# Batch 1's query path in a fused attention and feed-forward kernel: casts moved, columns as 64 by 64 tiles, batch 2's queries cast by GpSimd and turned at another place

## The chip, the cores and the metric

The kernel runs on one core of one Trainium2 chip. The metric is the time of one execution on the device in microseconds (us). Engines: PE is TensorE's matmul, PEld its weight load, DVE is VectorE, ACT is ScalarE, POOL is GpSimd, SPq is the queue from which transfers are issued.

## The reference

Per batch (8 batches, 8 heads, 576 rows, 64 columns a head): linear attention, a norm of each head's row, then a gated feed-forward with a norm ahead.

```python
kv  = einsum('bhsd,bhse->bhde', k, v)              # a 64x64 state per head
out = einsum('bhsd,bhde->bhse', q, kv)
out = out / sqrt(mean(out*out, -1) + 1e-6) * g_norm
x   = out.transpose(0, 2, 1, 3).reshape(4608, 512)
xn  = x / sqrt(mean(x*x, -1) + 1e-6) * rms_g
y   = (silu(xn @ w_gate) * (xn @ w_val)) @ w_out   # 512 -> 1536 -> 512
```

## The kernel before

The feed-forward of batch n and the attention of batch n+1 are interleaved on TensorE. The "up parts" are the products with w_gate and w_val, the "down parts" those with w_out. Between the up parts of batch 0 and those of batch 1, the rows of batch 1 have to be made: states from k and v, queries cast to bf16 and turned (by TensorE against an identity), columns (state times queries) for the sums of squares, row products, the norm, the row scalings, and a turn of the scaled rows. The down parts of batch 0 are placed between these steps to fill TensorE. The order, with cuts marked:

```python
for c in range(4):
    down_part(c, 0, 2)
att1.kv_products()                                   # states, diagonal 64x64 tiles
for i, engine in enumerate((DVE, SC)):
    cast_q(1, slice(2 * i, 2 * i + 2), engine)       # heads 0..3
att1.kv_copy()                                       # waits for the states
clear_tail_rows(1, DVE)
for i, engine in enumerate((DVE, SC)):
    cast_q(1, slice(2 * i + 4, 2 * i + 6), engine)   # heads 4..7
for c in range(4):
    down_part(c, 2, 4)
turns.q_turn(0, SC); turns.q_turn(1, DVE)            # 8 turns each, then a copy
# ... GpSimd casts of w_out
for c in range(2):
    down_part(c, 4, 6)
for j in range(NS):
    f_cols(j)             # one 128x128 matmul of 512 columns, then a square (ScalarE, j == 1 VectorE)
for c in range(2, 4):
    down_part(c, 4, 6)
F.alloc_sums(); F.sums(); f_o(0); F.head(); F.root() # sums, row products, Newton steps on VectorE
# ... down parts 6 to 8 with f_o(1..3) between
down_part(0, 8, 12)
xs = [F.scale(c, F.outa[c]) for c in range(4)]       # VectorE, both inputs in SBUF
ffn.down_out(0)
down_part(1, 8, 12)
f_x(0, xs[0], SC); f_x(1, xs[1], SC)                 # turns of the scaled rows
ffn.down_out(1)
alloc_q(2); cast_q(2, slice(0, 4), SC)               # batch 2's queries
down_part(2, 8, 12)
f_x(2, xs[2], DVE); f_x(3, xs[3], DVE)
down_part(3, 8, 12)
ffn.down_out(2); ffn.down_out(3)                     # the second one issues two stores
cast_q(2, slice(4, 8), DVE)
# ...
for c in range(T):
    atts[2].q_rows(c)                                # transposing transfers, in the queue after the stores
```

Of the kernel before, what the change touches and what calls it, by code (L numbers as in the profile page):

```python
# [10 lines left out]
FP32 = mybir.dt.float32  # L11
# [4 lines left out]
OP = mybir.AluOpType  # L16
ACT = mybir.ActivationFunctionType
# [3 lines left out]
def kernel(  # L21
# [14 lines left out]
    B, H, S, D = q.shape  # L36
    d_model = H * D
# [4 lines left out]
    T = 4  # L42
    MAIN = 128 * T
    TAIL = S - MAIN
    NS = d_model // 128
# [7 lines left out]
    def pool(name, bufs, **kw):  # L53
        return ctx.enter_context(tc.tile_pool(name=name, bufs=bufs, **kw))
# [13 lines left out]
    osb_pool = pool("osb", 2)  # L68

    PS = bass.MemoryType.PSUM  # L70
    gps_pool = pool("gps", 2, space=PS)
    vps_pool = pool("vps", 2, space=PS)
    ops_pool = pool("ops", 2, space=PS)
    att_pool = pool("att", 2, space=PS)
# [3 lines left out]
    PE, DVE, SC, GP = nc.tensor, nc.vector, nc.scalar, nc.gpsimd  # L78

    identity = consts.tile([128, 128], BF16, name="identity")  # L80
# [3 lines left out]
    gsq = consts.tile([128, 1], BF16, name="gsq")  # L84
    rowscale = consts.tile([128, NS], FP32, name="rowscale")
    sel = consts.tile([128, 2, 2], BF16, name="sel")
# [3 lines left out]
    kv_all = consts.tile([128, B, NS, 128], BF16, name="kv_all")  # L90
# [13 lines left out]
    def cast(engine, dst, src):  # L104
        if engine is SC:
            engine.copy(out=dst, in_=src)  # L106
        else:
            engine.tensor_copy(out=dst, in_=src)  # L108
# [35 lines left out]
    def cast_kv(b, name, i, engine):  # L144

        if b < EARLY:
            cast(engine, pairs_buf(b, name)[:, i].rearrange("p c d -> p (c d)"), pairs_raw(b, name)[:, i, :])
        elif i < NS:
            hs = slice(2 * i, 2 * i + 2)
            src = raws[b, name][:, 0 : MAIN * T].rearrange("p (h t d) -> p t h d", h=H, t=T)  # L150
            cast(engine, bufs[b][name][:, 0:T, hs, :], src[:, :, hs, :])
        else:
            src = raws[b, name][0:TAIL, MAIN * T :].rearrange("r (h d) -> r h d", h=H)
            cast(engine, bufs[b][name][0:TAIL, T], src)
# [10 lines left out]
    def alloc_q(b):  # L165
        bufs[b]["q"] = qb_pool.tile([128, T, H, D], BF16, name="qb")

    def cast_q(b, hs, engine):
        src = raws[b, "q"].rearrange("p (h t d) -> p t h d", h=H, t=T)[:, :, hs, :]
        cast(engine, bufs[b]["q"][:, :, hs, :], src)  # L170
# [48 lines left out]
    def round_wo(blk, i, n, engine):  # L219
        c = 4 * blk + i  # L220
        cast(engine, wo_sb[:, c : c + n, :], w_st["o", blk][:, i : i + n, :])
# [61 lines left out]
    def clear_tail_rows(i, engine):  # L283

        for t in (kbs[i], vbs[i]):
            engine.memset(t[TAIL:128, T], 0.0)
# [10 lines left out]
    class Att:  # L297
# [77 lines left out]
        def sums(self, c):  # L375
            if c == 0:
                self.ssq = stat_pool.tile([128, T, 2, H], FP32, name="ssq")
            sq = self.sq[c // 2][:, c % 2]
            DVE.tensor_tensor(out=sq[:, 1], in0=sq[:, 0], in1=gsq8, op=OP.mult)  # L379
            DVE.reduce_sum(out=self.ssq[:, c], in_=sq, axis=AX.X)  # L380
# [30 lines left out]
    class Cols:  # L411
# [11 lines left out]
                ps, lhsT=kv_all[:, self.n, j, :], rhs=self.qt[:, j, self.lo : self.hi], start=True, stop=True  # L423
            )

        def square(self, j, ps):
            SC.activation(out=self.sq[:, j, :], in_=ps, func=ACT.Square)

        def alloc_sums(self):
            self.bank = att_pool.tile([128, 512], FP32, name="att_ps")  # L430
            self.st = self.bank[:, 0 : self.nc * 2 * H].rearrange("p (c i h) -> p c i h", c=self.nc, i=2)

        def sums(self):
            for c in range(self.nc):
                PE.matmul(self.st[:, c, 0, :], lhsT=ones, rhs=epsrow, start=(c == 0), stop=False, skip_group_check=True)
            for j in range(NS):
                for c in range(self.nc):
                    PE.matmul(
                        self.st[:, c, :, 2 * j : 2 * j + 2], lhsT=self.sq[:, j, 128 * c : 128 * c + 128], rhs=sel,
                        start=False, stop=(j == NS - 1 and c == self.nc - 1), skip_group_check=True,  # L440
                    )

# [160 lines left out]
    for j in (0, 1):  # L603
# [5 lines left out]
        out=gam[NS : NS + 1, :].rearrange("o (i d) -> o i d", i=2),  # L609
        in_=g_norm.rearrange("(o d) -> o d", o=1).unsqueeze(1).to_broadcast([1, 2, D]),  # L610
# [83 lines left out]
    def rows_banks():  # L694
        return [ops_pool.tile([128, MAIN], FP32, name="o_ps") for _ in range(2)]
# [12 lines left out]
    for j in (0, 1):  # L708
# [24 lines left out]
    squares(A, 0, banksA[0])  # L733
    columns(A, 2, banksA[1])
    square(A, 2, banksA[1])
    kv3 = state0(3, 1)
    DVE.scalar_tensor_tensor(
        out=gsq, in0=gcol, scalar=1.0 / d_model, in1=gcol, op0=OP.mult, op1=OP.mult
# [5 lines left out]
    warm(A.bank, 1)  # L744
    columns(A, 3, banksA[1])
    square(A, 3, banksA[1])
    warm(A.bank, 1)
    A.sums()
# [64 lines left out]
    def broadcast_gsq():  # L813
        ps = att_pool.tile([128, 512], FP32, name="att_ps")
        PE.matmul(
            ps[:, 0:D], lhsT=gsq[0:D, :].to_broadcast([D, 128]), rhs=identity[0:D, 0:D], start=True, stop=True
        )
        DVE.tensor_copy(out=gsq8, in_=ps[:, 0:D].unsqueeze(1).to_broadcast([128, H, D]))

# [7 lines left out]
    for i in range(2):  # L827
        banks = [b.rearrange("p (u t) -> p u t", u=2) for b in rows_banks()] if i == 0 else None
        ffn.gate_pair(i, 256, ffn.up_pair(i, 256, banks=banks))
    broadcast_gsq()  # L830
    for s in range(2):
        round_w(3, "g", s, SC)
# [23 lines left out]
    turns = Turns(1)  # L856
# [22 lines left out]
        round_wo(0, i, 1, GP)  # L879
    alloc_xnt(1)  # L880

    def f_cols(j):
        p, nm = ((att_pool, "att_ps"), (att_pool, "att_ps"), (gps_pool, "g_ps"), (vps_pool, "v_ps"))[j]
        ps = p.tile([128, MAIN], FP32, name=nm)
        F.turned(j, ps)
        if j == 1:
            copy = osb_pool.tile([128, 2, d_model], FP32, name="o_sb")[:, 0, :]
            DVE.tensor_copy(out=copy, in_=ps)
            DVE.tensor_tensor(out=F.sq[:, j, :], in0=copy, in1=ps, op=OP.mult)
        else:  # L890
            SC.activation(out=F.sq[:, j, :], in_=ps, func=ACT.Square)

    def f_o(c):
        F.o(c, att_pool.tile([128, H, D], FP32, name="att_ps"), SC)

    def f_x(c, x, engine):
        bank = att_pool.tile([128, NS, 128], BF16, name="att_ps")
        to_rows(x, 1, c, bank, engine)

    pools = ("ops", "ops", "g", "v")  # L900

    def down_part(c, lo, hi):
        ffn.down_products(c, lo, hi, pools[c])
# [5 lines left out]
    for c in range(4):  # L909
        down_part(c, 0, 2)  # L910
    att1.kv_products()
    for i, engine in enumerate((DVE, SC)):
        cast_q(1, slice(2 * i, 2 * i + 2), engine)
    att1.kv_copy()
    clear_tail_rows(1, DVE)
    for i, engine in enumerate((DVE, SC)):
        cast_q(1, slice(2 * i + 4, 2 * i + 6), engine)
    for c in range(4):
        down_part(c, 2, 4)
    turns.q_turn(0, SC)  # L920
    turns.q_turn(1, DVE)
    for blk in (1, 2):
        for i in range(4):
            round_wo(blk, i, 1, GP)
    F = Cols(1, 0, 512, turns.qt, sqt_pool.tile([128, NS, MAIN], BF16, name="sqt"), "F")
    for c in range(2):
        down_part(c, 4, 6)
    for j in range(NS):
        f_cols(j)
    for c in range(2, 4):  # L930
        down_part(c, 4, 6)
    F.alloc_sums()
    F.sums()
    f_o(0)
    F.head()
    F.root()
# [11 lines left out]
    f_x(0, xs[0], SC)  # L948
    f_x(1, xs[1], SC)
    ffn.down_out(1)  # L950
    alloc_q(2)
    cast_q(2, slice(0, 4), SC)
    down_part(2, 8, 12)
    f_x(2, xs[2], DVE)
    f_x(3, xs[3], DVE)
    down_part(3, 8, 12)
    ffn.down_out(2)
    ffn.down_out(3)
    cast_q(2, slice(4, 8), DVE)



# [18 lines left out]

    cast_kv(2, "k", 0, DVE)
    cast_kv(2, "k", 1, DVE)
    atts = {b: Att(b) for b in range(2, B + 1)}
    for c in range(T):
        atts[2].q_rows(c)

    for n in range(1, B + 1):
        ffn = Ffn(n)
        steps = {u: [] for u in range(NF + T)}  # L990
# [9 lines left out]
        if n < B:  # L1000
# [5 lines left out]
            for i in range(2):  # L1006
                u = kv0 + 1 + 2 * i
# [9 lines left out]
        b = n + 2  # L1017
# [53 lines left out]
```

## Time and profile before

| | before |
|---|---|
| median, first three runs | 321.22 us (321.01 to 322.49) |
| span of the profiled run | 319.0 us |
| TensorE busy | 308.9 us, 97% of the span |
| TensorE in the chain that ended last | 87% |
| GpSimd busy | 22.8 us, 7% |

TensorE is busy nearly everywhere, so the busy shares show no place to gain. The way to read such a profile is to lay the starts of successive matmul groups side by side and to look for the places where one group starts later than the groups before it explain.

### The profile page before, as it was taken

What the parts mean: (1) busy time and instruction counts of PE and PEld (TensorE: products, weight loads), DVE (VectorE), ACT (ScalarE), POOL (GpSimd) and SP (SyncE); (2) the same over time, 40 slices, a digit from 0 to 9 for tenths busy, and PEclk for the clock granted to TensorE, in tenths of its full rate; (3) what the DMA queues carried; (4) which work ended last, traced back from release to release, by engine and by line L of the source; (5) the groups of instructions that cost most, each with busy time, mean ns of one, the idle gap of its engine ahead of it and who ended that gap; (6) DMA issues with size and microseconds to landing.
All of it is one profiled execution on the core that took longest, in us unless ns stands there. A gap on an engine that the chain in (4) does not pass through costs nothing.

```text
span 319.0 us, 5591 instructions
## 1 busy us (share of the span) xinstructions
PE 308.9 (97%) x2138; PEld 151.3 (47%) x2175; DVE 181.4 (57%) x372; ACT 176.6 (55%) x313; POOL 22.8 (7%) x48
## 2 busy tenths in 40 slices
PE   7899999999999999999999999999999999999995
PEld 3585456444454444444444444444444444444443
DVE  4685757669438922893279417951796079604310
ACT  3677457475667466837683767366744374233321
POOL 1274341300000000000000000000000000000000
PEclk9999999999999999999999999999999999999999
DMA  7999999888389757924792499946002600230014
GB/s 267 361 386 386 376 373 302 197 249 207 66 161 303 167 136 191 313 56 111 191 320 71 79 185 222 322 86 197 2 0 57 183 27 1 56 144 0 0 35 99
DMA packets 72903, 54.90 MB, mean 172 GB/s; under 512 B 42280, under 2 KB 64044, under 8 KB 72876
## 3 DMA queue, kind: packets, MB, share of 16 engines
q1 hardware_dynamic: 72496, 53.88, 60.4%
q10 hardware_dynamic: 380, 0.66, 0.6%
q8 instruction: 17, 0.28, 0.4%
q14 instruction: 10, 0.08, 0.1%
HBM read 37.75 MB, written 9.44 MB: 148 GB/s over the span
## 4 chain that ended last, share of the span: by engine, by line
PE 87%; DMA 6%; SPq 2%; issue 1%; DVE 1%; another core or an unknown queue 1%; ACT 1%; POOL 1%
PE v_ps L493 27%; PE g_ps L493 27%; PE o_ps L535 26%; DMA st<-in_moe_w_val_dram 3%; DMA st<-in_q_dram 2%; PE att_ps L278 1%; SPq L319 1%; DMA qt<-qb 1%; PE v_ps L535 1%; PE g_ps L535 1%; DMA out_dram<-o_sb 1%; POOL wv_sb L207 1%; PE o_ps L510 1%; PE att_ps L357 1%
## 5 line engine op out<-in xcount | busy, mean ns | idle before, releaser
L499 DVE TENSOR_TENSOR h_sb<-silu,v_ps 128x512 bf16<-128x512 bf16 x104 | 71.2, 684 | 98.7 <-ACT silu L498 66.7
L493 PE MATMUL v_ps<-xnt,wv_sb 128*128 128x512 bf16 x409 | 106.1, 379 | 0.6
L493 PE MATMUL g_ps<-xnt,wg_sb 128*128 128x512 bf16 x398 | 104.6, 379 | 0.8 <-ACT wg_sb L205 0.2
L498 ACT ACTIVATE silu<-g_ps 128x512 bf16<-128x512 f32 x104 | 62.1, 597 | 72.7 <-PE g_ps L493 57.7
L535 PE MATMUL o_ps<-wo_sb,h_sb 128*128 128x512 bf16 x386 | 86.9, 379 | 0.5
L493 PEld LDWEIGHTS <-wv_sb 128*128 128x128 bf16 x416 | 40.7, 98 | 49.1
L535 PEld LDWEIGHTS <-h_sb 128*128 128x128 bf16 x420 | 40.7, 98 | 47.8
L493 PEld LDWEIGHTS <-wg_sb 128*128 128x128 bf16 x416 | 39.6, 98 | 46.4
L106 ACT COPY o_sb<-o_ps 128x512 f32<-128x512 f32 (+1 forms) x34 | 19.7, 579 | 38.1 <-PE o_ps L535 35.3
L106 ACT CAST vb<-st 128x512 bf16<-128x512 f32 (+2 forms) x30 | 17.2, 628 | 3.3 <-DMA st<-in_v_dram 3.3
L397 DVE TENSOR_TENSOR xna<-outa,s1y 128x512 bf16<-128x512 bf16 x28 | 17.9, 685 | 0.0
L380 DVE TENSOR_REDUCE ssq<-sqt 128x16 f32<-128x1024 bf16 x14 | 17.1, 1220 | 0.5
L380 DVE TENSOR_REDUCE ssq<-sq 128x16 f32<-128x1024 bf16 x14 | 17.1, 1220 | 0.5
L106 ACT CAST qb<-st 128x1024 bf16<-128x1024 f32 (+1 forms) x17 | 15.4, 943 | 1.1 <-DMA st<-in_q_dram 1.1
L106 ACT CAST kb<-st 128x512 bf16<-128x512 f32 (+1 forms) x25 | 14.0, 619 | 0.0
L366 ACT ACTIVATE sq<-att_ps 128x512 bf16<-128x512 f32 x14 | 7.6, 594 | 4.3 <-PE att_ps L357 3.6
L379 DVE TENSOR_TENSOR sq<-sq,gsq 128x512 bf16<-128x512 bf16 x14 | 5.9, 422 | 4.9 <-ACT sq L366 4.9
L635 PE MATMUL att_ps<-kv_all 128*128 128x512 bf16 (+1 forms) x21 | 7.2, 467 | 1.2 <-DVE sel L624 1.2
L108 POOL CAST wo_sb<-st 128x512 bf16<-128x512 f32 x12 | 7.1, 620 | 7.9 <-DMA st<-in_moe_w_out_dram 7.9
L366 ACT ACTIVATE sqt<-o_ps 128x512 bf16<-128x512 f32 x14 | 7.6, 598 | 0.0
L371 ACT CAST outa<-att_ps 128x512 bf16<-128x512 f32 x14 | 7.5, 593 | 0.0
L371 ACT CAST outa<-o_ps 128x512 bf16<-128x512 f32 x14 | 7.5, 593 | 0.0
(145 smaller groups left out, 181.7 us busy)
## 6 DMA issues: line engine op xcount, KB each, us to landing
out_dram<-o_sb SPq DMA_DIRECT2D x14, 512.0 KB, 2.9
st<-in_q_dram SPq DMA_DIRECT2D x6, 1024.0 KB, 7.0
st<-in_k_dram SPq DMA_DIRECT2D x6, 1024.0 KB, 10.3
st<-in_v_dram SPq DMA_DIRECT2D x6, 1024.0 KB, 11.9
st<-in_moe_w_out_dram SPq DMA_DIRECT2D x6, 512.0 KB, 11.0
st<-in_moe_w_gate_dram SPq DMA_DIRECT2D x4, 512.0 KB, 9.6
st<-in_moe_w_val_dram SPq DMA_DIRECT2D x4, 512.0 KB, 8.8
st<-in_k_dram SPq DMA_DIRECT2D x4, 288.0 KB, 4.3
```

Of the source, the lines that this page charges most:

```text
L106: engine.copy(out=dst, in_=src)
L108: engine.tensor_copy(out=dst, in_=src)
L366: SC.activation(out=self.sq[i][:, :, 0, g:H:2, :], in_=self.banks[i][g], func=ACT.Square)
L371: SC.copy(out=rows[:, :, g:H:2, :], in_=self.banks[i][g])
L379: DVE.tensor_tensor(out=sq[:, 1], in0=sq[:, 0], in1=gsq8, op=OP.mult)
L380: DVE.reduce_sum(out=self.ssq[:, c], in_=sq, axis=AX.X)
L397: DVE.tensor_tensor(out=self.xna[c], in0=self.outa[c], in1=self.alpha[:, c, :].to_broadcast([128, H, D]), op=OP.mult)
L493: PE.matmul(ps, lhsT=wt[:, s, j * 128 : (j + 1) * 128], rhs=x[:, s, :], start=(s == 0), stop=(s == NS - 1),)
L498: SC.activation(out=silu, in_=g_ps, func=ACT.Silu)
L499: DVE.tensor_tensor(out=self.h[:, j, :], in0=silu, in1=v_ps, op=OP.mult)
L535: PE.matmul(self.o_ps[c], lhsT=self.h[:, j, c * 128 : (c + 1) * 128], rhs=wo_sb[:, j, :], start=(j == 0), stop=(j == NF - 1),)
L635: PE.matmul(ps[:, 0:w], lhsT=warm_sb[:, 0:128], rhs=warm_sb[:, 0:w], start=True, stop=True, skip_group_check=True)
```

## The change

It is meant to take out the small waits of TensorE around batch 1's rows: queries are cast before the state copies; the two query turns are put between down parts; the columns are made of 64 by 64 tiles, four of which are meant to run at once; batch 2's queries are cast by GpSimd, and their turning transfers go ahead of the last two stores. Cut to its core:

```diff
+        def turned_tiles(self, i, banks):
+            for u in range(2):
+                out = slice(u * D, u * D + D)
+                for g in range(2):
+                    rows = slice(g * D, g * D + D)
+                    PE.matmul(banks[g][out], lhsT=kv_all[rows, self.n, 2 * i + u, rows],
+                              rhs=self.qt[rows, 2 * i + u, :], start=True, stop=True)
 ...
-    for i, engine in enumerate((DVE, SC)):
+    for i, engine in enumerate((DVE, SC, DVE, SC)):
         cast_q(1, slice(2 * i, 2 * i + 2), engine)
     att1.kv_copy()
     clear_tail_rows(1, DVE)
-    for i, engine in enumerate((DVE, SC)):
-        cast_q(1, slice(2 * i + 4, 2 * i + 6), engine)
-    for c in range(4):
-        down_part(c, 2, 4)
-    turns.q_turn(0, SC)
-    turns.q_turn(1, DVE)
     for blk in (1, 2):
         for i in range(4):
             round_wo(blk, i, 1, GP)
+    alloc_q(2)
+    for i in range(2):
+        cast_q(2, slice(4 * i, 4 * i + 4), GP)
+    down_part(0, 2, 4)
+    turns.q_turn(0, SC)
+    down_part(1, 2, 4)
+    turns.q_turn(1, DVE)
+    for c in range(2, 4):
+        down_part(c, 2, 4)
-    for c in range(2):
-        down_part(c, 4, 6)
-    for j in range(NS):
-        f_cols(j)
-    for c in range(2, 4):
+    for i in range(2):
+        f_cols(i)
+    for c in range(4):
         down_part(c, 4, 6)
 ...
-    alloc_q(2)
-    cast_q(2, slice(0, 4), SC)
     down_part(2, 8, 12)
     f_x(2, xs[2], DVE)
     f_x(3, xs[3], DVE)
     down_part(3, 8, 12)
+    atts = {b: Att(b) for b in range(2, B + 1)}
+    for c in range(T):
+        atts[2].q_rows(c)
     ffn.down_out(2)
     ffn.down_out(3)
-    cast_q(2, slice(4, 8), DVE)
```

The rest of the diff fits the squares, the order of heads in the sums and the one-matmul gamma broadcast to this.

More of the change, by code (lines that the diff above doesn't have):

```diff
@@ L424, in turned @@
             )
-        def square(self, j, ps):
-            SC.activation(out=self.sq[:, j, :], in_=ps, func=ACT.Square)
+        def turned_tiles(self, i, banks):
[3 more added lines that the diff above has]
+                    rows = slice(g * D, g * D + D)
+                    PE.matmul(
+                        banks[g][out], lhsT=kv_all[rows, self.n, 2 * i + u, rows], rhs=self.qt[rows, 2 * i + u, :],
+                        start=True, stop=True,
+                    )
         def alloc_sums(self):
@@ L431, in alloc_sums, with sums @@
             self.st = self.bank[:, 0 : self.nc * 2 * H].rearrange("p (c i h) -> p c i h", c=self.nc, i=2)
-        def sums(self):
+        def sums(self, heads=lambda j: slice(2 * j, 2 * j + 2)):
             for c in range(self.nc):
@@ L438, in sums @@
                     PE.matmul(
-                        self.st[:, c, :, 2 * j : 2 * j + 2], lhsT=self.sq[:, j, 128 * c : 128 * c + 128], rhs=sel,
+                        self.st[:, c, :, heads(j)], lhsT=self.sq[:, j, 128 * c : 128 * c + 128], rhs=sel,
                         start=False, stop=(j == NS - 1 and c == self.nc - 1), skip_group_check=True,
@@ L815, in broadcast_gsq @@
         PE.matmul(
-            ps[:, 0:D], lhsT=gsq[0:D, :].to_broadcast([D, 128]), rhs=identity[0:D, 0:D], start=True, stop=True
+            ps[:, 0:D], lhsT=gsq.to_broadcast([128, 128]), rhs=identity[:, 0:D], start=True, stop=True
         )
@@ L880, with f_cols, f_heads @@
     alloc_xnt(1)
-    def f_cols(j):
-        p, nm = ((att_pool, "att_ps"), (att_pool, "att_ps"), (gps_pool, "g_ps"), (vps_pool, "v_ps"))[j]
-        ps = p.tile([128, MAIN], FP32, name=nm)
-        F.turned(j, ps)
-        if j == 1:
-            copy = osb_pool.tile([128, 2, d_model], FP32, name="o_sb")[:, 0, :]
-            DVE.tensor_copy(out=copy, in_=ps)
-            DVE.tensor_tensor(out=F.sq[:, j, :], in0=copy, in1=ps, op=OP.mult)
-        else:
-            SC.activation(out=F.sq[:, j, :], in_=ps, func=ACT.Square)
+    def f_cols(i):
+        pools = ((att_pool, "att_ps"),) * 2 if i == 0 else ((gps_pool, "g_ps"), (vps_pool, "v_ps"))
+        banks = [p.tile([128, MAIN], FP32, name=nm) for p, nm in pools]
+        F.turned_tiles(i, banks)
+        for g in range(2):
+            sq = F.sq[:, 2 * i + g, :]
+            if i == 0 and g == 1:
+                copy = osb_pool.tile([128, 2, d_model], FP32, name="o_sb")[:, 0, :]
+                DVE.tensor_copy(out=copy, in_=banks[g])
+                DVE.tensor_tensor(out=sq, in0=copy, in1=banks[g], op=OP.mult)
+            else:
+                SC.activation(out=sq, in_=banks[g], func=ACT.Square)
+    def f_heads(j):
+        h = 4 * (j // 2) + j % 2
+        return slice(h, h + 3, 2)
     def f_o(c):
@@ L924 @@
             round_wo(blk, i, 1, GP)
-    F = Cols(1, 0, 512, turns.qt, sqt_pool.tile([128, NS, MAIN], BF16, name="sqt"), "F")
-    for c in range(2):
-        down_part(c, 4, 6)
-    for j in range(NS):
-        f_cols(j)
-    for c in range(2, 4):
+    alloc_q(2)
[7 more added lines that the diff above has]
+        down_part(c, 2, 4)
+    F = Cols(1, 0, 512, turns.qt, sqt_pool.tile([128, NS, MAIN], BF16, name="sqt"), "F")
+    for i in range(2):
+        f_cols(i)
+    for c in range(4):
         down_part(c, 4, 6)
     F.alloc_sums()
-    F.sums()
+    F.sums(f_heads)
     f_o(0)
@@ L983 @@
     cast_kv(2, "k", 1, DVE)
-    atts = {b: Att(b) for b in range(2, B + 1)}
-    for c in range(T):
-        atts[2].q_rows(c)
     for n in range(1, B + 1):
```

## The prediction

> **What bounds the kernel now.** I read the page first, then the chain of waits in order of time, then the timelines of the engines between 38 and 67 us, where the changed lines run. The page says who sets the time:
>
> ```profile
> PE 308.9 (97%) x2138; PEld 151.3 (47%) x2175; DVE 181.4 (57%) x372; ACT 176.6 (55%) x313; POOL 22.8 (7%) x48
> PE 87%; DMA 6%; SPq 2%; issue 1%; DVE 1%; another core or an unknown queue 1%; ACT 1%; POOL 1%
> ```
>
> The first line is busy time by engine, the second is the chain that ended last. The matmul engine is busy for 97% of the span and is 87% of the chain; its clock is full everywhere. So only what shortens or delays the matmul stream counts. Work saved on VectorE, ScalarE or GpSimd is worth nothing unless a matmul waits for it. The matmul stream in the changed stretch (PE timeline: start, length, instructions; ends are modelled, so I take differences of starts):
>
> ```profile
> 42.34 1.04 PE L535 MATMUL o_ps<-wo_sb,h_sb 128*128 128x512 bf16 x3
> 44.08 1.35 PE L848 MATMUL att_ps<-identity,qb 128*128 128x128 bf16 x16
> 45.27 1.03 PE L535 MATMUL o_ps<-wo_sb,h_sb 128*128 128x512 bf16 x4
> 46.22 0.60 PE L422 MATMUL att_ps<-qt,kv_all 128*128 128x512 bf16 x2
> 47.09 0.59 PE L535 MATMUL g_ps<-wo_sb,h_sb 128*128 128x512 bf16 x2
> 47.95 0.24 PE L435 MATMUL att_ps<-epsrow,ones 128*128 128x8 bf16 x4
> 48.65 0.38 PE L446 MATMUL att_ps<-kv_all,qt 128*128 128x128 bf16 x4
> 52.99 0.61 PE L291 MATMUL att_ps<-identity,xna 128*128 128x128 bf16 x8
> 55.62 1.03 PE L493 MATMUL g_ps<-xnt,wg_sb 128*128 128x512 bf16 x3
> ...
> 65.21 0.41 PE L357 MATMUL att_ps<-kv_all,qt 64*128 64x64 bf16 x16
> 66.09 0.29 PE L357 MATMUL o_ps<-kv_all,qt 64*128 64x64 bf16 x8 [0.36 <-DMA qt<-qb]
> 66.31 1.04 PE L493 MATMUL g_ps<-xnt,wg_sb 128*128 128x512 bf16 x4
> ```
>
> Between 55.62 and 65 nearly everything is at 0.216 us for a 512-column matmul (0.86 us for four). The losses are small: the 16 query turns take 1.19 us (44.08 to 45.27), where 8 such turns take 0.45 us in line L291 (52.99 to 53.44, the next start), and the L357 block waits for the last transfer that turns batch 2's queries. The weight-load timeline names the first wait, the chain of waits shows that the matmuls of the norm sums (L438) stood until VectorE's square was there:
>
> ```profile
> 44.47 0.78 PEld L848 LDWEIGHTS <-qb 128*128 128x128 bf16 x14 [0.29 <-DVE qb L108]
> 48.30 0.03 issue
> 48.33 0.45 PE att_ps L438 x12
> ```
>
> **What the Trainium skill says.** "TensorEngine Tiling (Array Packing)", Tiling Modes: 64 by 64 tiles make four independent arrays, and a change of tiling mode drains the engine. "TensorE: Matmul & The Clock Gate", Part 3: tiles on different row and column groups run at once, with a few ns between starts. The trace has tiles two at a time: 16 row-tiled L357 matmuls take 0.24 us (65.21 to 65.45), 15 ns each, where 64 columns at 216 ns per 512 are 27 ns. It shows no four at a time. The drain is visible as about 0.1 us: the tiled block at 65.21 follows four matmuls that began at 64.25 and are due to end at 65.11. "SBUF — State Buffer", Who interferes with whom: GpSimd and VectorE share a port pair as an exclusive lock; a VectorE cast in a two-port mode, and also a VectorE instruction with two SBUF inputs against a GpSimd read, blocks fully until the other's instruction is over. The trace agrees for casts:
>
> ```profile
> 55.39 0.68 DVE L108 CAST qb<-st 128x1024 bf16<-128x1024 f32 x1
> 55.99 1.17 DVE L108 CAST kb<-st 128x512 bf16<-128x512 f32 x2
> 55.59 0.96 POOL L108 CAST kb<-st 64x512 bf16<-64x512 f32 x1 [6.74 <-DMA st<-in_k_dram]
> ```
>
> GpSimd's cast takes 0.96 us where the others of 512 columns take about 0.61; the first of the two VectorE casts after it takes 0.83 us where 0.42 is usual. They took turns. For two SBUF inputs no such overlap is in this trace.
>
> **The change, part by part.**
>
> 1. Batch 1's query casts move ahead of the state copies. Before, the last VectorE cast ran at 43.85 to 44.41, behind the state copy that waits for the state products. After, all four can run from 40.2 to about 41.5: the second half of the queries was issued at 28.04 and takes about 12.5 us, so it has landed by 40.6. The products end at 42.34, so the copies are not held up. Gain: the 0.29 us wait.
>
> 2. The turns go between the down parts. From 42.34: 0.43 down, 0.45 turn, 0.43 down, 0.45 turn, 0.86 down, so the matmul engine is at 44.96. ScalarE's copy of the first turn (1.01 us from 43.4) is done at 44.4, VectorE's of the second (0.69 us from about 44.3) at 45.0. The wait before the columns stays at about 0.1 us, as it is now. Neither gain nor loss.
>
> 3. Columns as tiles: now 0.95 us (46.14, where the four downs end, to 47.09). Eight tiles as two groups of four at 0.216 us are 0.43 us, plus the 0.1 us wait and 0.1 us for each of two mode changes, some of it under the wait: about 0.65 us. Gain about 0.3 us.
>
> 4. All eight down matmuls of parts 4 to 6 now stand between columns and sums, so 1.73 us instead of 0.86 us for the squares. VectorE's copy and product (0.69 us each, from 45.5) end at 46.9, the sums begin at about 47.3. They wait no more: from 0.70 us (47.95 to 48.65) to about 0.5 us, since the 10 matmuls of the same kind of batch 0 take 0.25 us (17.09 to 17.34). Gain 0.2 us. So at the sums the stream is about 0.29 + 0.3 + 0.2 = 0.8 us ahead. The gamma broadcast (one matmul, now over 128 rows, of which 64 meet zeros of the identity) costs the same.
>
> 5. Batch 2's queries turned sooner: four transposes stand ahead of the last two stores in the queue. Before, they were issued from 58.81 to 64.82, the last landing at 66.05. The L357 block takes 1.10 us (65.21 to 66.31); the same block of the next batch, which waits for nothing, takes 0.65 us (94.90 to 95.55). Issued about 2 us sooner they are in time: gain 0.45 us.
>
> 6. The casts of batch 2's queries leave ScalarE (1.07 us) and VectorE (0.68 us). No matmul waited for them: gain 0. They go to GpSimd, two of 1024 columns. From 0.61 us at 512 and 0.67 at 576 columns I estimate 1.06 us each. They start when the queries land: issued at 37.94, 12.7 us, so 50.64. This is where it can go wrong, since VectorE then runs the four row scalings, of two SBUF inputs each:
>
> ```profile
> 51.52 2.50 DVE L474 TENSOR_TENSOR xna<-outa,F1y 128x512 bf16<-128x512 bf16 x4
> ```
>
> Moved 0.8 us ahead they begin at 50.7, at the same moment.
>
> Sum without interference: 0.8 + 0.45 = 1.25 us, some 320.0 us.
>
> **The rivals.**
>
> First, the shared port. If the scalings and the GpSimd casts take turns, both need 2.5 + 2.1 = 4.6 us from 50.7, and the fourth scaling ends at about 55.3 whichever starts. After it come its turn (0.22 us) and the last down part (0.86 us), so the next feed-forward starts at about 56.5 instead of 55.62: a loss of 0.9 us in place of the gain of 0.8 us. The earlier transposes still give 0.45 us back. Time about 321.65 us. For it: the casts of this trace took turns, and the skill's page names two SBUF inputs. Against it: no overlap of just this kind in the trace, and the landing time can shift. If GpSimd gets only one cast in between, the loss is 1.06 us shorter: about 320.6 us.
>
> Second, the tiles do not run four at a time: two at a time cost 0.87 us plus mode changes, so part 3 loses 0.1 instead of gaining 0.3, and the total is 0.4 us worse: 320.4 us without the port's conflict. For it: this trace shows pairs alone. Against it: four share no quarter of the array, and the two groups of rows write different banks.
>
> Third, all hidden: the next wait (the scalings' chain, which now has 0.8 us of slack at the first turn and 0.4 us at the second) eats the gain of parts 1 to 4, and only the 0.45 us of the transposes remain: 320.8 us. Against it: the chain of small VectorE operations starts with the sums and moves ahead with them.
>
> **Range and chances.** I give 45% to the port's conflict (321.3 to 321.9), 20% to a part of it or to one of the other two (320.4 to 320.9), 35% to the clean gain (319.7 to 320.3). The weighted mean is about 320.7 us, which I predict although it lies between the two main cases. The three runs of before spread from 321.01 to 322.49, so I take 319.6 to 322.0. Two per cent are 6.4 us; nothing here is a quarter of that. Faster by over 2%: 0.01; within: 0.98; slower: 0.01.
>
> **What would show it.** Part 1: no wait for a query cast in the weight loads of the turns, which take 0.45 us each. Part 3: columns in about 0.65 us, four matmuls starting within some 50 ns of each other. Part 4: the sums in 0.5 us. Part 5: no wait for the transfer at the L357 block, which takes 0.65 us. Part 6: GpSimd's query casts from 50.7; with the conflict, scalings of over 1 us with those casts between them and a wait of the turns (L291) for them; without, 0.63 us each and the feed-forward from 54.8. Wrong in size: a landing well off 50.6, or a wait that I have not named in the later batches, whose matmul stream I take as unchanged.

## The result, and the profile after

| | before | changed |
|---|---|---|
| median of 6 runs, first job | 321.62 us (321.01 to 322.49) | 321.03 us (320.60 to 321.71) |
| ratio, first job | | 0.9981, interval 0.9961 to 1.0001 |
| ratio, second job (run e8 below) | | 1.0001, interval 0.9988 to 1.0015 |
| span of the profiled run | 319.0 us | 319.5 us |

A ratio is worked out from the fast runs of both kernels in the same job, so it is not quite the ratio of the medians quoted; the interval is one of 95%. Executions over 1.5% slower than the fastest of the same kernel are left out of the means. The change is within noise of nothing. The busy times and the chain look as they did (the first line of part 1 of the page and the first of part 4):

```profile
PE 311.2 (97%) x2179; PEld 151.1 (47%) x2179; DVE 182.2 (57%) x371; ACT 176.1 (55%) x312; POOL 24.8 (8%) x50
PE 89%; DMA 4%; DVE 2%; SPq 2%; ACT 1%; issue 0%; DVEq 0%
```

One difference matters here: VectorE is in the chain with 2% where it had 1%. The matmul timeline of the changed kernel (start, length, line, instructions; line numbers have moved: L856 are the query turns that were L848, L432 the tiled columns that were L422, L443 and L446 the sums that were L435 and L438, L454 the row products that were L446) shows where both the gain and the loss are:

```profile
42.46 0.61 PE L543 MATMUL o_ps<-wo_sb,h_sb 128*128 128x512 bf16 x2
42.90 0.61 PE L856 MATMUL att_ps<-identity,qb 128*128 128x128 bf16 x8
43.35 0.59 PE L543 MATMUL o_ps<-wo_sb,h_sb 128*128 128x512 bf16 x2
...
45.18 0.41 PE L432 MATMUL att_ps<-qt,kv_all 64*64 64x512 bf16 x4
45.42 0.38 PE L432 MATMUL g_ps<-qt,kv_all 64*64 64x512 bf16 x1
...
45.43 0.38 PE L432 MATMUL v_ps<-qt,kv_all 64*64 64x512 bf16 x1
45.74 1.04 PE L543 MATMUL o_ps<-wo_sb,h_sb 128*128 128x512 bf16 x4
...
47.48 0.24 PE L443 MATMUL att_ps<-epsrow,ones 128*128 128x8 bf16 x4
47.98 0.38 PE L454 MATMUL att_ps<-kv_all,qt 128*128 128x128 bf16 x4
...
53.16 0.40 PE L291 MATMUL att_ps<-identity,xna 128*128 128x128 bf16 x4 [0.67 <-DVE xna L482]
53.76 0.40 PE L291 MATMUL att_ps<-identity,xna 128*128 128x128 bf16 x4 [0.21 <-DVE xna L482]
56.17 1.03 PE L501 MATMUL g_ps<-xnt,wg_sb 128*128 128x512 bf16 x4
65.75 0.41 PE L357 MATMUL att_ps<-kv_all,qt 64*128 64x64 bf16 x16
66.33 1.04 PE L501 MATMUL g_ps<-xnt,wg_sb 128*128 128x512 bf16 x4
```

Up to 47.98 everything is shorter: a turn takes 0.44 us, the columns end at 45.74, the sums take 0.50 us, the batch 2 block takes 0.58 us (65.75 to 66.33). But the turns of the scaled rows (L291) now wait for VectorE. Its timeline and GpSimd's say why:

```profile
50.33 0.19 DVE L245 SCALAR_TENSOR_TENSOR F1c<-F1a,Fz 128x32 f32<-128x32 f32 x1
50.56 1.06 DVE L247 SCALAR_TENSOR_TENSOR F1y<-F1c,F0y 128x32 f32<-128x32 f32 x1
51.72 3.19 DVE L482 TENSOR_TENSOR xna<-outa,F1y 128x512 bf16<-128x512 bf16 x4
50.53 2.02 POOL L108 CAST qb<-st 128x1024 bf16<-128x1024 f32 x2 [1.94 <-DMA st<-in_q_dram]
```

The last Newton step takes 1.06 us where its twin takes 0.19. (Six such VectorE steps, 32 columns wide, refine the reciprocal square root of the norm.) It began just after GpSimd's first cast and ended with it: the casts take 1.04 us each, and the first ran from 50.53 to 51.57. The four scalings take 3.19 us instead of 2.50.

To compare runs I cut the span at four starts of the matmul timeline, all in us. "Opening" is the start of the state products L270. "A" is from there to the first row product, "B" from there to the first up matmul of batch 1, "block 2" and "block 3" are the L357 blocks of batches 2 and 3 (first start to the start of the next group), "tail" is from the start of VectorE's last copy to the end of the span. Everything between is the same to 0.01 or 0.02 us in all these traces.

| run | opening | A | B | block 2 | block 3 | tail | span |
|---|---|---|---|---|---|---|---|
| before | 41.08 | 7.57 | 6.97 | 1.10 | 0.65 | 3.82 | 319.0 |
| changed | 41.20 | 6.78 | 8.19 | 0.58 | 0.84 | 4.11 | 319.5 |
| e1 casts back | 41.04 | 6.78 | 6.97 | 0.57 | 0.68 | 3.75 | 317.6 |
| e2 GpSimd only | 42.22 | 7.62 | 8.46 | 0.57 | 0.57 | 4.15 | 321.4 |
| e3 sooner only | 41.96 | 7.44 | 6.98 | 0.57 | 0.58 | 3.77 | 319.1 |
| e4 batch 1's part | 41.16 | 7.08 | 6.98 | 0.93 | 0.57 | 3.77 | 318.3 |
| e5 writes only | 40.93 | 6.78 | 6.98 | 0.57 | 0.60 | 3.84 | 317.5 |
| e6 whole columns | 42.25 | 7.08 | 6.97 | 0.57 | 0.61 | 3.82 | 319.1 |
| e7 sooner in all batches | 41.38 | 6.78 | 6.98 | 0.58 | 0.57 | 3.81 | 317.9 |
| e8 changed again | 41.04 | 6.78 | 8.27 | 0.57 | 0.58 | 4.06 | 319.1 |

The first two rows account for the result: A gives 0.79 us, block 2 gives 0.52 us, B takes 1.22 us, block 3 takes 0.19 us, the tail 0.29 us and the opening 0.12 us. The sum is 0.51 us more, and the span is 0.5 us longer. The opening swings by 1.3 us between runs in which its code does the same, so single times say little, and the sections say much. A itself is 7.57, 7.62 and 7.44 us in the three runs with the old order of batch 1 (before, e2, e3), and 6.78 us in five of the six with the whole new one. The sixth is e4, with 7.08 us, for a reason given there.

### The profile page after: what moved, and what is told of

Its sections match the earlier page's. It is cut to its first block, busy times and chain, and to the rows that moved or that the text cites. A ratio compares the mean times of both kernels' runs of the same rounds, so it can differ in the third digit from the quotient of the medians.

```text
span 319.5 us, 5632 instructions
## 1 busy us (share of the span) xinstructions
PE 311.2 (97%) x2179; PEld 151.1 (47%) x2179; DVE 182.2 (57%) x371; ACT 176.1 (55%) x312; POOL 24.8 (8%) x50
## 4 chain that ended last, share of the span: by engine, by line
PE 89%; DMA 4%; DVE 2%; SPq 2%; ACT 1%; issue 0%; DVEq 0%
PE g_ps L501 28%; PE v_ps L501 27%; PE o_ps L543 25%; DMA st<-in_v_dram 2%; SPq L319 2%; DMA st<-in_k_dram 1%; PE att_ps L278 1%; PE v_ps L518 1%; PE g_ps L518 1%; DMA qt<-qb 1%; PE att_ps L270 1%; PE g_ps L543 1%; PE v_ps L543 1%; DMA out_dram<-o_sb 1%; DVE xna L482 1%; PE o_ps L518 1%
## 5 line engine op out<-in xcount | busy, mean ns | idle before, releaser
L501 PE MATMUL g_ps<-xnt,wg_sb 128*128 128x512 bf16 x416 | 106.9, 379 | 0.0
L543 PE MATMUL o_ps<-wo_sb,h_sb 128*128 128x512 bf16 x396 | 87.8, 379 | 0.0
L543 PEld LDWEIGHTS <-h_sb 128*128 128x128 bf16 x420 | 40.6, 98 | 47.7 <-issue 0.4
L106 ACT CAST qb<-st 128x1024 bf16<-128x1024 f32 (+1 forms) x16 | 14.4, 935 | 1.9 <-DMA st<-in_q_dram 1.9
L643 PE MATMUL att_ps<-kv_all 128*128 128x512 bf16 (+1 forms) x23 | 8.4, 491 | 1.2 <-DVE sel L632 1.2
L108 DVE CAST kb<-st 128x576 bf16<-128x576 f32 (+1 forms) x12 | 5.9, 512 | 3.0 <-DMA st<-in_k_dram 2.9
```

The costliest lines, as they stand in the source:

```text
L106: engine.copy(out=dst, in_=src)
L108: engine.tensor_copy(out=dst, in_=src)
L501: PE.matmul(ps, lhsT=wt[:, s, j * 128 : (j + 1) * 128], rhs=x[:, s, :], start=(s == 0), stop=(s == NS - 1),)
L543: PE.matmul(self.o_ps[c], lhsT=self.h[:, j, c * 128 : (c + 1) * 128], rhs=wo_sb[:, j, :], start=(j == 0), stop=(j == NF - 1),)
L643: PE.matmul(ps[:, 0:w], lhsT=warm_sb[:, 0:128], rhs=warm_sb[:, 0:w], start=True, stop=True, skip_group_check=True)
```

## The experiments

My theory after the result: batch 1's part works as meant, and GpSimd's casts give it back by holding VectorE up. The rival: the gain is hidden by any next wait, and GpSimd only happened to be there. Each experiment is given as its change against the kernel named, cut to its core, with comments added; each is correct against the reference. They ran in two jobs (e1 to e4, then e5 to e8), each beside the kernel before.

### e1: casts back on ScalarE and VectorE (against the changed kernel)

```diff
-    alloc_q(2)
-    for i in range(2):
-        cast_q(2, slice(4 * i, 4 * i + 4), GP)
 ...
     ffn.down_out(1)
+    alloc_q(2)
+    cast_q(2, slice(0, 4), SC)
     down_part(2, 8, 12)
     f_x(2, xs[2], DVE)
     f_x(3, xs[3], DVE)
+    cast_q(2, slice(4, 8), DVE)
```

> The changed kernel with one thing undone: the two casts of batch 2's queries go back from GpSimd to ScalarE and VectorE, at their old places; the four transposes stay ahead of the last two stores. Theory (GpSimd's casts hold the port that the last Newton step and the row scalings need): no wait before the turns L291, the last Newton step takes 0.19 us and the four scalings 2.5 us, the next feed-forward starts about 1.2 us sooner than in the changed kernel against the start of the sums, and the L357 block still takes 0.65 us. Time about 1.2 us under the kernel before, ratio 0.996. Rival (the gain of the matmul stream is hidden by something else anyway): the turns wait again for something, ratio 0.998 to 0.999, as the changed kernel.

VectorE's cast stands one step sooner than in the kernel before, since the transfers that need it now stand sooner too.

Measured: 320.31 us median beside 321.17, ratio 0.9971 (0.9953 to 0.9988). Its VectorE and matmul timelines:

```profile
50.39 0.19 DVE L247 SCALAR_TENSOR_TENSOR F1y<-F1c,F0y 128x32 f32<-128x32 f32 x1
50.69 2.50 DVE L482 TENSOR_TENSOR xna<-outa,F1y 128x512 bf16<-128x512 bf16 x4
...
52.16 0.61 PE L291 MATMUL att_ps<-identity,xna 128*128 128x128 bf16 x8
54.79 1.03 PE L501 MATMUL g_ps<-xnt,wg_sb 128*128 128x512 bf16 x4
```

The step is 0.19 us again, the scalings 2.50, and no wait stands before the turns. B is 6.97 us as before the change, A stays at 6.78 and block 2 at 0.57. So no other wait eats the gain, and the rival falls. The sections promise 0.79 + 0.53 = 1.3 us, a ratio of 0.996, which the interval holds. That e1 is faster than the changed kernel is read from the sections: the two were not run in the same job, and their ratios' intervals overlap. (e7 and e8 below, of one job, show it in time as well.)

### e2: the GpSimd casts alone (against the kernel before)

```diff
             round_wo(blk, i, 1, GP)
+    alloc_q(2)
+    for i in range(2):
+        cast_q(2, slice(4 * i, 4 * i + 4), GP)
 ...
-    alloc_q(2)
-    cast_q(2, slice(0, 4), SC)
 ...
-    cast_q(2, slice(4, 8), DVE)
```

> The kernel before with one thing changed: batch 2's queries are cast by GpSimd instead of ScalarE and VectorE; transposes, columns, turns and casts of batch 1 as before. Theory of the port: GpSimd's two casts of 1.01 us run from about 50.6 to 52.6 us; two of the small Newton steps of VectorE are stretched from 0.19 to about 1 us each, the scalings end 1.5 us later than before, the turns L291 wait, the feed-forward starts 0.8 to 1.1 us later; ratio about 1.003. Rival (the stretched operations of the changed kernel come from its new order, not from GpSimd): no stretched operation, ratio 1.000.

Measured: 321.85 us beside 321.17, ratio 1.0026 (1.0005 to 1.0046). VectorE and GpSimd in this run:

```profile
51.52 0.95 DVE L245 SCALAR_TENSOR_TENSOR F0c<-F0a,Fz 128x32 f32<-128x32 f32 x1
52.50 0.95 DVE L247 SCALAR_TENSOR_TENSOR F0y<-F0c,Fyi 128x32 f32<-128x32 f32 x1
53.49 0.19 DVE L243 TENSOR_TENSOR F1a<-F0y 128x32 f32<-128x32 f32 x1
51.39 2.02 POOL L108 CAST qb<-st 128x1024 bf16<-128x1024 f32 x2 [1.95 <-DMA st<-in_q_dram]
```

The two stretched steps end where the two casts end, at about 52.4 and 53.4, and the steps after are normal. Without any of the new columns the casts alone add 1.49 us to B. This is the cleanest sight of the mechanism. Block 2 waits for nothing here, which makes up for part of the loss in the time: the delay in B put the stream further behind the transfers, which were issued from 60.40, 7.5 us before the block at 67.89, and in the kernel before only 6.4 us before it (58.81 and 65.21).

### e3: the turning transfers sooner, alone (against the kernel before)

```diff
     f_x(3, xs[3], DVE)
+    cast_q(2, slice(4, 8), DVE)
     down_part(3, 8, 12)
+    atts = {b: Att(b) for b in range(2, B + 1)}
+    for c in range(T):
+        atts[2].q_rows(c)
     ffn.down_out(2)
     ffn.down_out(3)
-    cast_q(2, slice(4, 8), DVE)
```

> The kernel before with one thing changed: the four transposes of batch 2's queries stand ahead of the last two stores in the queue (the casts stay on ScalarE and VectorE, VectorE's just ahead of the last down part). Theory: the last transpose lands about 2 us sooner, the L357 block takes 0.65 us instead of 1.10, all else the same: 0.45 us gained, ratio 0.9986. Rival (the later matmuls wait for something else in its place): block 0.65 us but a new wait after it, ratio 1.000.

Measured: 320.95 us beside 321.17, ratio 0.9997 (0.9980 to 1.0015), which can't tell 0.45 us from nothing. The trace can: block 2 takes 0.57 us instead of 1.10, B is 6.98 us, and nothing after it is longer. As sections go, this part is worth 0.53 us.

### e4: batch 1's part alone (against the changed kernel)

```diff
-    alloc_q(2)
-    for i in range(2):
-        cast_q(2, slice(4 * i, 4 * i + 4), GP)
 ...    (casts and transposes of batch 2 back as in the kernel before)
```

> The changed kernel without its part for batch 2: query casts of batch 1 ahead of the state copies, turns between down parts and columns as 64 by 64 tiles stay; batch 2's queries are cast and turned as in the kernel before. Theory: sums end 0.8 us sooner against the end of the state products, scalings 2.5 us, no wait before the turns; the feed-forward 0.8 us sooner; the L357 block waits for its transfer as before, if the stores and transposes move with the stream (1.1 us), or a little longer. Ratio 0.9975 to 0.998. Rival (gain hidden): feed-forward not sooner, ratio 1.000.

Measured: 319.94 us beside 321.17, ratio 0.9963 (0.9949 to 0.9978). B is 6.98 us: the gain isn't hidden. But A is 7.08 us, not 6.78. The reason is in its weight-load and ScalarE timelines:

```profile
43.12 0.47 PEld L856 LDWEIGHTS <-qb 128*128 128x128 bf16 x6 [0.17 <-DVE qb L108]
42.65 0.62 ACT L106 CAST qb<-st 128x512 bf16<-128x512 f32 x1 [0.83 <-DMA st<-in_q_dram]
```

In this run the second half of batch 1's queries landed only at about 42.6, and the first turn, moved ahead by the change, had to wait for its cast. In the changed kernel's profile it landed at about 41.9, just soon enough. Block 2 takes 0.93 us, as the transfers move with the stores: the gain of columns and that of transposes are separate. The sections of this profile promise 0.49 + 0.17 us, less than the times show; with the queries landing in time they would promise 0.3 us more. The profiled run is also the slowest of the five (320.57 us, with a span 0.6 to 0.8 us longer than the others). The interval is 0.7 to 1.6 us in time, so 0.66 lies just outside and 0.96 inside; I take the sections for the cause and the time for the sign. In the same job e4 (319.94 us) is no slower than e1 (320.31), though e1 has the transposes' gain besides: the times don't confirm what the transposes are worth, only the sections do.

### e5: GpSimd only writes (against e1)

```diff
+    filler = consts.tile([128, 512], BF16, name="filler")
 ...
+    GP.tensor_copy(out=filler[:, 0:1], in_=raws[2, "q"][:, 0:1])
+    for i in range(6):
+        GP.memset(filler, 0.0)
     down_part(0, 2, 4)
     turns.q_turn(0, SC)
```

> As e1_casts_back, and GpSimd does something else when batch 2's queries land: one copy of a single column (which waits for the landing), then six memsets of 128x512 bf16 into a spare tile, which read no SBUF and are needed by nobody. Theory, as the Trainium skill's page SBUF - State Buffer has it (two SBUF inputs of VectorE contend only with a GpSimd instruction that reads): the Newton steps stay at 0.19 us and the four scalings at 2.5 us though the memsets lie beside them, no wait before the turns L291; from the first matmul of row products to the feed-forward 6.97 us, as in e1_casts_back. Rival (any GpSimd work holds the port): stretched Newton steps or scalings and 7.3 us or more.

Measured: one look, 319.26 us, state not told. VectorE and GpSimd:

```profile
50.29 0.19 DVE L248 SCALAR_TENSOR_TENSOR F1y<-F1c,F0y 128x32 f32<-128x32 f32 x1
50.59 2.52 DVE L483 TENSOR_TENSOR xna<-outa,F1y 128x512 bf16<-128x512 bf16 x4
50.83 3.44 POOL L936 MEMSET filler<- 128x512 bf16 x6
```

All but the first 0.24 us of the scalings lies beside the memsets, and they take 2.52 us; B is 6.98 us. So it isn't GpSimd's being at work that stretches VectorE. The casts of e2 read SBUF and the memsets don't, but they are also another and a longer operation, so e5 alone doesn't show that reading is what counts. That the Newton steps would also be free was not tried here: the memsets came just after them.

The other side, VectorE's inputs, can be read from e1's trace. There GpSimd's casts of w_out, which do read SBUF, lie beside two earlier steps of VectorE's chain:

```profile
48.39 0.19 DVE L231 TENSOR_TENSOR Ft<-Fr,att_ps 128x32 f32<-128x32 f32 x1
48.83 0.19 DVE L235 SCALAR_TENSOR_TENSOR Fz<-Fm,att_ps 128x32 f32<-128x32 f32 x1
47.89 1.17 POOL L108 CAST wo_sb<-st 128x512 bf16<-128x512 f32 x2 [0.77 <-DMA st<-in_moe_w_out_dram]
```

These steps are of the same kinds and width as the stretched ones, but one of their two inputs (att_ps) lies in PSUM, and they take 0.19 us. So a GpSimd cast does not hold up every VectorE step beside it: the stretched ones have both inputs in SBUF.

### e6: whole columns again (against e1)

```diff
-    for i in range(2):
-        f_cols(i)                 # eight 64x64 tiles
+    for j in range(NS):
+        f_cols(j)                 # four 128x128 matmuls, as before
 ...
-    F.sums(f_heads)
+    F.sums()
```

> As e1_casts_back, with batch 1's columns as four 128x128 matmuls again and the sums in their order; casts, turns and down parts as changed. Theory: the columns take 0.95 us instead of 0.65 us, so from the start of the state products to the first row product 7.08 us instead of 6.78; the sums still take 0.5 us because all eight down parts stand before them. Rival (the tiles only move a wait): 6.8 us.

Measured: one look, 321.34 us, with an opening of 42.25, the latest of all. A is 7.08 us, 0.30 more than e1; B and block 2 as in e1, and the sums take 0.51 us. The tiles themselves are worth 0.30 us, and the other 0.49 us of A come from casts, turns and sums.

### e7: transposes sooner in the later batches too (against e1)

```diff
-                steps[13].append(lambda b=b, c=c: atts[b].q_rows(c))
+                steps[12].append(lambda b=b, c=c: atts[b].q_rows(c))
```

> As e1_casts_back, and the query transposes of the later batches stand ahead of the first store of their batch too (one step sooner). This is the candidate for the best version. Theory: the small waits for the transfer at batch 3's L357 block (block 0.68 us in e1_casts_back, 0.84 in the changed kernel, 0.57 where nothing waits) go, block 0.57; all else as e1_casts_back. Ratio 0.996 to 0.997, the 0.1 us not to be told from e1_casts_back by times. Rival (the later stores now hold up something): a new wait or a longer rest.

Measured: 319.91 us beside 321.40, ratio 0.9953 (0.9941 to 0.9966). Block 3 is 0.57 us, and no section is longer by more than these sections differ elsewhere. That the edit took the wait of block 3 away is not shown: e2, e3, e4 and e8 have 0.57 or 0.58 us there without it. It was run in another job than e1, so the two ratios don't rank them; by sections it is 0.1 us better in this one profile. It is clearly faster than the kernel before, and, in the same job, than the changed kernel (e8, 321.39 us).

### e8: the changed kernel once more

> The changed kernel once more, to see how much the collision moves from run to run. Theory: stretched last Newton step or scalings again where GpSimd's query casts (from the landing, 50 to 52.7 us) meet them; the stretch from the first row product to the feed-forward 7.5 to 8.5 us against 6.97 without a collision; L357 block of batch 2 without a wait. Ratio 0.998 to 1.000. Rival (a chance of the one profile): no stretched operation, 6.97 us, ratio 0.996.

Measured: 321.39 us beside 321.40, ratio 1.0001 (0.9988 to 1.0015). B is 8.27 us, but in another way than the first time:

```profile
50.47 0.19 DVE L247 SCALAR_TENSOR_TENSOR F1y<-F1c,F0y 128x32 f32<-128x32 f32 x1
50.76 4.17 DVE L482 TENSOR_TENSOR xna<-outa,F1y 128x512 bf16<-128x512 bf16 x4
51.21 2.58 POOL L108 CAST qb<-st 128x1024 bf16<-128x1024 f32 x2 [1.95 <-ACT outa L106]
```

Here the queries landed some 0.7 us later: issued at 38.29, they took 12.8 us instead of 12.0. (The line names as releaser a cast of ScalarE on another tile, which ended at the same moment.) The Newton step was free, the first scaling was under way before GpSimd's first cast, the casts took 2.58 us instead of 2.02 (they waited as well), and the four scalings 4.17 us instead of 2.50. Taken one by one they take turns: a scaling ended at 51.45, a cast at 52.35, a scaling at 52.89, a cast at 53.79, a scaling at 54.34 and the last at 54.94. Whoever comes first, the turns wait for both.

## Why the prediction was right or wrong

The time was right: 320.7 us was predicted, 321.03 measured, inside the range of 319.6 to 322.0. This is in good part luck. The range covered nearly every course, and 320.7 was a weighted mean that none of the cases would give; with the middles of the three bands it comes to 320.85, not 320.7. The measured 321.03 lies between two bands, beside a kernel before whose median was now 321.62 and not the 321.22 of the first three runs. By its steps:

1. **Query casts ahead of the state copies.** The gain came, but the step "so it has landed by 40.6" was wrong. The second half was cast from 41.94 in the changed kernel, after a wait of 0.85 us for its transfer, and from 42.65 in e4, where it cost 0.3 us of A. The error is one of reading: the 12.5 us belong to the first half, issued at 27.58. Asked for the second issue alone (`--dma --window 29:31`), the profile gives no time to landing. In the changed kernel 13.5 us lie between that issue (28.4) and the cast. Why it takes longer, whether because the issue itself lasts 4.36 us or otherwise, was not tested.

2. **Turns between down parts: right.** Each turn group takes 0.44 us (42.90 to 43.35), and the wait before the columns is 0.09 us (45.09, when the downs end, to 45.18).

3. **Columns as tiles: right in mechanism and size.** From 45.09 to 45.74 they take 0.65 us with the wait, as predicted; the last four start within 0.01 us (45.42 to 45.43). e6 isolates the gain: 0.30 us. The rival "two at a time" falls.

4. **Sums without a wait: right.** 0.50 us (47.48 to 47.98). That the sums had waited for VectorE's square is not in the chain's lines that the prediction shows; the square's end at 48.28, just before the sums went on at 48.33, bears it out. Parts 1 to 4 together gave 0.79 us, with 0.8 predicted.

5. **Transposes sooner: right in mechanism, a little larger.** 0.53 us instead of 0.45. The mis-sized term is the free block: I took 0.65 us from batch 3 as one that waits for nothing, but blocks that wait for nothing take 0.57 us (e3, and batches 4 to 7 of every trace).

6. **GpSimd's casts.** The first rival, the shared port, is what happens. Its size was too large: "a loss of 0.9 us in place of the gain of 0.8 us" needs B to grow by 1.7 us, and it grew by 1.22 and 1.30. The mis-sized term is the 4.6 us for casts and scalings together: where they did take turns one by one (e8), they took 4.17 us. In the changed kernel's profile the first cast fell on a Newton step, and only one scaling was held up (3.19 instead of 2.50 us); the fourth scaling ended at 54.91, not 55.3, on a clock that ran 0.12 us late. This loss of 1.22 to 1.30 us cancels the 1.3 us that batch 1's part and the transposes gain together.

The third rival ("all hidden") is refuted by e1 and e4: B is 6.97 to 6.98 us whenever GpSimd does not read. What I did not foresee are block 3 in the first profile, 0.84 us, in the second 0.58 (a transfer that lands in the nick of time), and the tail.

That GpSimd's casts cause the loss is shown: undone it goes (e1), done alone it comes (e2), repeated it stays (e8). That it is a matter of GpSimd reading SBUF is supported by e5 for the scalings, but not isolated, and that it is a matter of VectorE's two SBUF inputs by the steps with one input in PSUM. That the port is locked for the whole instruction rests on the ends in e2, where each stretched step ends with a cast, on the turns in e8, and on the Trainium skill's page "SBUF — State Buffer", Who interferes with whom.

## What to carry to other kernels

Moving a cast to an engine that is 93% idle is not free if that engine shares a port with one that has a chain of short operations with two SBUF inputs to run just then: a 0.19 us step took 0.95 to 1.06 us. Before moving work to GpSimd, look at when its input lands and what VectorE does in the two microseconds after it; an engine on whose work nothing waits just then, here ScalarE, may be the better place (e1). And where the opening of a kernel swings by more than the change is worth, compare sections between matmul starts, not spans.

## What the Trainium skill lacked or had wrong

- "SBUF — State Buffer", Who interferes with whom: right on two SBUF inputs against GpSimd's reads, and that writes alone don't contend (e2: two steps of 0.95 us instead of 0.19; e5: four scalings in 2.52 us beside 3.44 us of memsets). It names `tensor_tensor`; e2 shows `scalar_tensor_tensor` with two SBUF inputs held up the same way, which the section's general rule covers without naming it. It gives no example with small operations: here one of 0.19 us took 0.95 to 1.06 us, since it waited for most of a GpSimd cast of 1.04 us.
- "TensorEngine Tiling (Array Packing)", Key Properties: says that a change of tiling mode drains the engine, but gives no time. Here the weight loads after the tiled columns stood for 0.41 us, of which the matmul stream lost little: the tiled block of two groups took 0.56 us (45.18 to 45.74) where two groups of 512 columns are 0.43. No run isolates the mode change as the reason.
- No page has it: in the three profiles with GpSimd query casts the tail is 4.06 to 4.15 us, in the seven others 3.75 to 3.84. GpSimd had been idle for 250 us by then, and e5, which gives it even more instructions, has 3.84. The cause stays open.
